# Down sums of three token blocks of a fused layer with the weights stationary and 512 tokens moving, their result transposed by DMA

## The chip, the cores and the metric

The kernel runs on one core of one Trainium2 chip. The metric is the device time of one execution in microseconds; lower is better. A profile also gives the *span*, from the first to the last recorded instruction of the core. The time is a little longer than the span, and that difference, which I call the *time outside the span*, becomes important below.

The engines are called PE (the matrix engine; "PEld" is its weight load), DVE (vector), ACT (activation), POOL and SP (which here mostly issues DMAs); SPq, ACTq and POOLq stand for these engines issuing DMAs. The trace also shows the clock that PE was granted, as a fraction of full speed.

Single executions of one kernel scatter by some tenths of a microsecond. A run is called slow when its granted clock is low; only fast runs, at granted clock 1.0 (two at 0.999), are compared in time here.

## The reference

For 2048 tokens of 640 channels, a layer norm feeds two branches, whose sum is added to the input:

```python
xn = _layernorm(x, axis=-1)
return x + _A_ref(xn, A_wqkv, A_wo) + _B_ref(xn, B_w_gate, B_w_up, B_w_down)

# _A_ref: 32 heads of 20 channels, each token attends to 8 tokens at distances 0, 2, ... 14; then @ wo
# _B_ref:
g = jnp.einsum("bsd,df->bsf", x, w_gate)      # 640 -> 1536
u = jnp.einsum("bsd,df->bsf", x, w_up)
return jnp.einsum("bsf,fd->bsd", g * u, w_down)   # 1536 -> 640
```

The last matrix products of both branches, `@ wo` (contraction 640, five pieces of 128) and `w_down` (contraction 1536, twelve pieces of 128), are summed in one accumulation of 17 matmuls. These are the *down sums*.

## The kernel before

All large products run on PE in bf16. Activations lie transposed in SBUF (channels on partitions, tokens along the free dimension). The down sums want their result with tokens on partitions, as the output in memory has it, so the kernel keeps a piece of 128 tokens of the activations stationary and moves 320 columns of the weights:

```python
# constants: TS = 128 (token tile), JB = 512 (token block), NF = 12, NCH = 5, DHALF = 320, TLAST = 12
def tail(t, nb):                      # tile t of 16, half nb of the 640 output channels
    j, rows = t // 4, slice((t % 4) * TS, (t % 4 + 1) * TS)
    flush_h(0)
    n = NF + NCH
    # ... (the very last half is cut into 192 + 128 columns)
        for i in range(n):
            if i < NF:
                l, x = ht(j, i)[:, rows], WD[:, i, cols]
            else:
                l, x = VO[:, i - NF, t * TS:(t + 1) * TS], WO[:, i - NF, cols]
            op("pe", ... e.matmul(PS[:, b, 0:wid], l, x, start=(i == 0), stop=(i == n - 1)) ...)
        if t < TLAST:
            if nb == 0:
                fin_bank[0] = b
                continue
            # both halves evicted together by ACT, fp16
            op("act", ... e.activation(o, i, ACT.Copy) ...)        # FACC <- PS, 128x640
            continue
        # tiles 12 to 15: DVE adds the input x and stores
    if nb == 1 and t < TLAST:
        if t % 2 == 0:
            return
        # two tiles together are added to the output in memory, which already holds a copy of x
        stores.append(op("pool", lambda e: e.dma_start(d, f, accum_op=ALU.add), ...))
```

A small layer in the kernel records every operation with what it reads and writes and derives all waits from that. Each DMA gets a semaphore of its own. The order of PE's work is a fixed list; a down sum of tile `t` is put behind the value block (the weighted sum of the attention, 256 tokens each, on DVE) that it reads:

```python
def add_dn(j):
    for t in range(4 * j, 4 * j + 4):
        for nb in range(2):
            fill.append(("dn", t // 2, 2.31, lambda t=t, nb=nb: tail(t, nb)))

add_gu(0); add_gu(1); add_gu(2)      # gate and up sums of a block of 512 tokens
add_dn(0); add_gu(3); add_dn(1); add_dn(2); add_dn(3)
```

Of the kernel before, what the change touches and what calls it, by code (L numbers as in the profile page):

```python
# [5 lines left out]
FP16 = mybir.dt.float16  # L6
ACT = mybir.ActivationFunctionType
ALU = mybir.AluOpType

S = 2048  # L10
D = 640
NCH = 5
# [3 lines left out]
NF = 12  # L16
W = 8
# [3 lines left out]
NJ = 4  # L21
TS = 128
JB = 512
# [6 lines left out]
SB = 256  # L30
NSB = HS // SB
# [10 lines left out]
class Sched:  # L42
# [50 lines left out]
    def op(self, eng, fn, r=(), w=(), dma=False, name="", group=None):  # L93
        X = _Op()
        X.eng, X.fn, X.name, X.dma = eng, fn, name, dma
        X.needs_tick, X.event, X.pre_know, X.idx = False, None, None, len(self.ops)
        rk = [k for a in r for k in self.keys(a)]
        wk = [k for a in w for k in self.keys(a)]
        deps = {}
        inorder = eng in ("pe", "act", "dve")  # L100
        for k in rk:
            st = self.state.get(k)
            if st is not None:
                for o in st[0]:
                    deps[o.idx] = o
        for k in wk:
            st = self.state.get(k)
            if st is None:
                continue
            if group is not None and st[2] == group and not st[1]:  # L110
                for o in st[3]:
                    deps[o.idx] = o
                continue
            for o in st[0]:
                if not (eng == "pe" and o.eng == "pe"):
                    deps[o.idx] = o
            for q in st[1]:
                if eng in ("pe", "act") and q.eng == eng and not q.dma:
                    continue
                deps[q.idx] = q  # L120
        last = {}
        keep = []
        for d in deps.values():
            if d.dma or d.eng == "pool":
                keep.append(d)
            else:
                b = last.get(d.eng)
                if b is None or b.idx < d.idx:
                    last[d.eng] = d
        X.deps = keep + list(last.values())  # L130
        for d in X.deps:
            if not d.dma:
                d.needs_tick = True
        for k in rk:
            st = self.state.get(k)
            if st is None:
                self.state[k] = [[], [X], None, []]
            elif inorder and st[1] and st[1][-1].eng == eng and not st[1][-1].dma:
                st[1][-1] = X
            else:  # L140
                st[1].append(X)
        for k in wk:
            st = self.state.get(k)
            if group is not None and st is not None and st[2] == group and not st[1]:
                st[0].append(X)
            else:
                before = [] if st is None else st[0] + st[1]
                self.state[k] = [[X], [], group, before]
        if dma:
            X.event = (self.nc.alloc_semaphore(f"dma{self.n_dma}"), 16)  # L150
            self.n_dma += 1
        self.ops.append(X)
        return X
# [59 lines left out]
def build_kernel(nc, A_x, A_wqkv, A_wo, B_x, B_w_gate, B_w_up, B_w_down, out):  # L213
    K = Sched(nc)
    op = K.op

    place = [16512]

    def sb(name, shape, dtype=BF16, at=None):
        n = mybir.dt.size(dtype)  # L220
        for s in shape[1:]:
            n *= s
        n = (n + 63) // 64 * 64
        if at is None:
            at = place[0]
            place[0] += n
        assert at + n <= 229344, (name, at + n)
        return K.sbuf(name, shape, dtype, at)
# [4 lines left out]
    WD = sb("WD", [128, NF, D])  # L233
    WO = sb("WO", [128, NCH, D])
# [9 lines left out]
    VO = sb("VO", [128, NCH, VP + S])  # L244
    QH, KH, ATB = [], [], []
# [25 lines left out]
    TLAST = 12  # L271
    XR = sb("XR", [128, NXR, D])
    NFO = 4
    FOUT = sb("FOUT", [128, NFO, D])
    FACC = sb("FACC", [128, NFO, D], FP16, at=place[0] - NFO * D * 2)
    NUS = 7
    a_us = place[0]
    USX = sb("USX", [128, NUS, JB])
# [9 lines left out]
    PS = nc.alloc_psum_tensor("PS", [128, 8, 512], FP32)  # L288
    xhbm = A_x[0]
    ohbm = out[0]  # L290

    def dma(o, i, r=(), w=(), name="", eng="sp", group=None):
        return op(eng, lambda e: e.dma_start(o, i), r=r, w=w, dma=True, name=name, group=group)
# [6 lines left out]
                                         fill=1.0, base=0, channel_multiplier=1),  # L300
       r=[IDENT[:]], w=[IDENT[:]], name="ident")
# [156 lines left out]
    def bank():  # L458
        b = bank_ring.pop(0)
        bank_ring.append(b)  # L460
        return b
# [164 lines left out]
    def flush_h(keep):  # L626
        n = 0
        while len(h_pending) > keep:
            h_pending.pop(0)()
            n += 1  # L630
        return n

    def ht(j, m):
        if j != 2:
            return HT[:, j % 3 % 2, m, :]
        if m < 2 * NCH:
            return XNT[:, m % NCH, m // NCH * JB:(m // NCH + 1) * JB]
        return HX[:, m - 2 * NCH, :]
# [19 lines left out]
    def xr_load(t):  # L658
        dma(XR[:, t % NXR, :], xhbm[t * TS:(t + 1) * TS, :], w=[XR[:, t % NXR, :]], name=f"xr{t}")

    stores = []
    fin_bank = [0]

    def tail(t, nb):
        j, rows = t // 4, slice((t % 4) * TS, (t % 4 + 1) * TS)
        flush_h(0)
        n = NF + NCH
        last = t == NT - 1
        parts = ((0, DHALF - 128), (DHALF - 128, 128)) if last and nb == 1 else ((0, DHALF),)
        for h, wid in parts:  # L670
            b = bank()
            c0 = nb * DHALF + h
            cols = slice(c0, c0 + wid)
# [4 lines that stand above are left out]
                    l, x = VO[:, i - NF, t * TS:(t + 1) * TS], WO[:, i - NF, cols]  # L678
                op("pe", (lambda l, x, i, b, wid: lambda e: e.matmul(PS[:, b, 0:wid], l, x, start=(i == 0), stop=(i == n - 1)))(l, x, i, b, wid),  # L679
                   r=[l, x], w=[PS[:, b, :]], name=f"dn{t}_{nb}_{i}")  # L680
            if t < TLAST:
                if nb == 0:
                    fin_bank[0] = b
                    continue
                assert b == fin_bank[0] + 1
                o = FACC[:, t % NFO, :].rearrange("p (n d) -> p n d", n=2)
                i = PS[:, b - 1:b + 1, 0:wid]
                op("act", (lambda o, i: lambda e: e.activation(o, i, ACT.Copy))(o, i),  # L688
                   r=[PS[:, b - 1, :], PS[:, b, :]], w=[o], name=f"fin{t}")
                continue  # L690
            o = FOUT[:, t % NFO, cols]
            xr = XR[:, t % NXR, cols]
            op("dve", (lambda o, xr, b, wid: lambda e: e.tensor_tensor(o, PS[:, b, 0:wid], xr, ALU.add))(o, xr, b, wid),  # L693
               r=[PS[:, b, :], xr], w=[o], name=f"fin{t}_{nb}")
            if last:
                eng = "act" if c0 == DHALF else "sp"
                stores.append(dma(ohbm[t * TS:(t + 1) * TS, cols], o, r=[o], name=f"odma{t}_{c0}", eng=eng))
        if nb == 1 and t < TLAST:
            if t % 2 == 0:
                return  # L700
            f = FACC[:, (t - 1) % NFO:(t - 1) % NFO + 2, :]
            d = ohbm[(t - 1) * TS:(t + 1) * TS, :].rearrange("(u p) n -> p u n", p=TS)
            stores.append(op("pool", lambda e: e.dma_start(d, f, accum_op=ALU.add), r=[f, ("out",)], w=[("out", t)],  # L703
                             dma=True, name=f"oacc{t}"))
        elif nb == 1 and not last:
            f = FOUT[:, t % NFO, :]
            stores.append(dma(ohbm[t * TS:(t + 1) * TS, :], f, r=[f], name=f"odma{t}"))
            if t + NXR < NT:
                xr_load(t + NXR)
# [84 lines left out]
    for which, t in ((0, 4), (1, 4), (0, 5), (1, 5)):  # L794
        b = bank()
# [19 lines left out]
    fill, pos = [], [0]  # L815
# [16 lines left out]
            fill.append((1.08, lambda m=m: glu(1, m, j)))  # L832

    def add_dn(j):
        for t in range(4 * j, 4 * j + 4):
            for nb in range(2):
                fill.append(("dn", t // 2, 2.31, lambda t=t, nb=nb: tail(t, nb)))

    add_gu(0)
    add_gu(1)  # L840
    add_gu(2)
    add_dn(0)
    add_gu(3)
    add_dn(1)
    add_dn(2)
    add_dn(3)

# [102 lines left out]
def bass_parallel_sum__sliding_local_dilated__glu_gated_bilinear__prompt_kernel(  # L950
    nc, A_x, A_wqkv, A_wo, B_x, B_w_gate, B_w_up, B_w_down, out
):
    build_kernel(nc, A_x, A_wqkv, A_wo, B_x, B_w_gate, B_w_up, B_w_down, out)
# [28 lines left out]
```

## Time and profile before

| | kernel before |
|---|---|
| time, fast runs at the start | 254.13 us median (253.92 to 254.18, 3 runs) |
| span of the profiled run, granted clock | 375.0 us, 0.658 (a slow run) |
| PE, DVE, ACT busy in it | 371.7, 219.0, 114.5 us |

The profile is of an execution in which PE was granted about 0.65 of its clock for almost the whole span. It shows the order of things and the durations of the other engines (ACT's 128x512 evictions took 597 ns in it; DVE was busy 219.0 us in it), but PE's times have to be rescaled.

These are lines from the page of the kernel before: busy time and share of the span for each engine with the number of instructions, the granted clock in tenths over 40 slices, and the chain of work that ended last, by engine.

```profile
span 375.0 us, 3825 instructions
## 1 busy us (share of the span) xinstructions
PE 371.7 (99%) x1572; PEld 184.2 (49%) x1572; DVE 219.0 (58%) x255; ACT 114.5 (31%) x202; POOL 35.8 (10%) x44
...
PEclk8666666666666666666666666666666666666666
...
## 4 chain that ended last, share of the span: by engine, by line
PE 99%; DVE 0%; issue 0%
```

PE is the chain: 99% of the span is PE work that follows directly on PE work. Whatever is to shorten the kernel has to shorten that stream.

The same chain in order of time (start in us, length in us, what, number of matmuls). L489 are 128-column matmuls, L648 the gate and up sums with 512 columns, L679 the down sums with mostly 320.

```profile
23.43 8.12 PE PS L489 x100
...
105.00 117.50 PE PS L648 x360
222.50 27.81 PE PS L679 x136
250.31 39.17 PE PS L648 x120
289.48 83.23 PE PS L679 x425
```

The 360 matmuls of 512 took 326.4 ns each, the first 136 of 320 took 204.5 ns each: nearly the same time per column.

Two groups of the kernel before, by form (line, engine, operation, tiles, shapes, count | busy us, mean ns | idle time before, and what ended it): a weight load of the down sums and their eviction.

```profile
L679 PEld LDWEIGHTS PS<-WD,HT 128*128 128x128 bf16 x300 | 35.5, 120 | 24.1 <-issue 0.9
...
L688 ACT ACTIVATE FACC<-PS 128x640 f16<-128x640 f32 x12 | 8.4, 703 | 73.3 <-PE PS L679 73.3
```

### The profile page before, as it was taken

To read this page: it belongs to the slowest core of one execution; us is meant where nothing else is said; L and a number is where in the kernel's file an instruction comes from. 1 tells how busy PE (TensorE), PEld (TensorE's weight loads), DVE (VectorE), ACT (ScalarE), POOL (GpSimd) and SP (SyncE) were. 2 spreads that over 40 slices of the span, in tenths; PEclk is the share of its full clock that TensorE was granted. 3 is DMA by queue.
4 is the path that set the end of the run, shared out by engine and by line. 5 is a ranking of instruction groups with operands and counts; after the bars stand their busy time and mean duration, and the time that the engine had idled before them with its cause. 6 is when DMAs were issued, how large, how long until landed. Compare 5 with 4: busy or idle time off the path is not lost.

```text
span 375.0 us, 3825 instructions
## 1 busy us (share of the span) xinstructions
PE 371.7 (99%) x1572; PEld 184.2 (49%) x1572; DVE 219.0 (58%) x255; ACT 114.5 (31%) x202; POOL 35.8 (10%) x44
## 2 busy tenths in 40 slices
PE   8999999999999999999999999999999999999997
PEld 5998544444433333333333346553334556556555
DVE  5766899992017238967666432997846998000111
ACT  4544443333333344333333332113333001001000
POOL 0000012344000300111100000110000010010000
PEclk8666666666666666666666666666666666666666
DMA  7754696766100412453991000612000020220411
GB/s 218 217 115 84 181 361 148 129 120 120 20 0 2 92 20 82 149 107 71 251 344 18 0 1 0 180 80 35 2 0 0 0 37 0 35 37 0 72 35 35
DMA packets 25664, 31.83 MB, mean 85 GB/s; under 512 B 9872, under 2 KB 22160, under 8 KB 25616
## 3 DMA queue, kind: packets, MB, share of 16 engines
q1 hardware_dynamic: 19120, 22.16, 18.3%
q0 software_dynamic: 6240, 9.31, 15.7%
q8 instruction: 12, 0.20, 0.2%
q10 hardware_dynamic: 288, 0.13, 0.1%
q14 instruction: 4, 0.03, 0.0%
HBM read 14.42 MB, written 4.59 MB: 51 GB/s over the span
## 4 chain that ended last, share of the span: by engine, by line
PE 99%; DVE 0%; issue 0%
PE PS L648 42%; PE PS L679 30%; PE PS L474 17%; PE PS L509 4%; PE PS L502 2%; PE PS L489 2%; PE PS L452 1%; PE PS L433 0%; DVE FOUT L693 0%; DVE ZERO L296 0%; DVE EPSC L297 0%
## 5 line engine op out<-in xcount | busy, mean ns | idle before, releaser
L648 PE MATMUL PS<-XNT,WU 128*128 128x512 bf16 x240 | 87.3, 513 | 0.0
L648 PE MATMUL PS<-XNT,WG 128*128 128x512 bf16 x240 | 87.3, 513 | 0.0
L474 PE MATMUL PS<-XNT,WQKV 128*128 128x512 bf16 x200 | 65.4, 513 | 0.0
L679 PE MATMUL PS<-WD,HT 128*128 128x320 bf16 (+2 forms) x300 | 63.4, 382 | 0.0
L648 PEld LDWEIGHTS PS<-XNT,WG 128*128 128x128 bf16 x240 | 29.3, 122 | 48.8 <-issue 48.7
L648 PEld LDWEIGHTS PS<-XNT,WU 128*128 128x128 bf16 x240 | 29.0, 121 | 49.3 <-issue 49.3
L679 PEld LDWEIGHTS PS<-WD,HT 128*128 128x128 bf16 x300 | 35.5, 120 | 24.1 <-issue 0.9
L653 DVE TENSOR_TENSOR HT<-HT,USX 128x512 bf16<-128x512 bf16 x36 | 15.2, 422 | 54.8 <-ACT USX L650 54.8
L474 PEld LDWEIGHTS PS<-XNT,WQKV 128*128 128x128 bf16 x200 | 26.9, 135 | 38.0 <-issue 37.7
L615 DVE TENSOR_TENSOR PVB<-VO,ATB 128x10240 f16<-128x10240 bf16 x8 | 43.9, 5488 | 0.2
L650 ACT ACTIVATE USX<-PS 128x512 bf16<-128x512 f32 x48 | 28.6, 597 | 48.7 <-PE PS L648 47.7
L679 PE MATMUL PS<-WO,VO 128*128 128x320 bf16 (+2 forms) x165 | 38.8, 384 | 0.0
L610 DVE TENSOR_TENSOR PVB<-PVB 128x5120 f16<-128x5120 f16 (+1 forms) x16 | 34.5, 2155 | 0.3
L693 DVE TENSOR_TENSOR FOUT<-PS,XR 128x320 bf16<-128x320 f32 (+2 forms) x9 | 4.1, 454 | 51.7 <-PE PS L679 51.7
L650 ACT ACTIVATE HT<-PS 128x512 bf16<-128x512 f32 x36 | 21.5, 597 | 36.4 <-PE PS L648 36.4
L688 ACT ACTIVATE FACC<-PS 128x640 f16<-128x640 f32 x12 | 8.4, 703 | 73.3 <-PE PS L679 73.3
L543 POOL DMA_DIRECT2D LOG<-PE x24 | 21.9, 925 | 58.0 <-DMA LOG<-PE 58.0
L679 PEld LDWEIGHTS PS<-WO,VO 128*128 128x128 bf16 x165 | 19.7, 121 | 13.0
L703 POOL DMA_DIRECT2D out_dram<-FACC x6 | 7.1, 1186 | 141.9 <-ACT FACC L688 141.9
L532 DVE TENSOR_TENSOR PP<-QH,KH 128x2048 f16<-128x2048 bf16 x16 | 19.1, 1218 | 0.0
L532 DVE TENSOR_TENSOR TMP<-QH,KH 128x2048 f16<-128x2048 bf16 x16 | 19.0, 1218 | 0.0
L537 DVE TENSOR_TENSOR PP<-PP,TMP 128x4096 f16<-128x4096 f16 x8 | 18.3, 2289 | 0.2
(67 smaller groups left out, 250.6 us busy)
## 6 DMA issues: line engine op xcount, KB each, us to landing
PE<-PP POOLq DMA_DIRECT2D x8, 512.0 KB, 4.8
ATB<-LOG SPq DMA_DIRECT2D x8, 512.0 KB, 4.8
LOG<-PE POOLq DMA_DIRECT2D x24, 128.0 KB, 2.7
WG<-in_B_w_gate_dram SPq DMA_DIRECT2D x1, 1920.0 KB, 9.1
WU<-in_B_w_up_dram SPq DMA_DIRECT2D x1, 1920.0 KB, 15.8
WD<-in_B_w_down_dram SPq DMA_DIRECT2D x1, 1920.0 KB, 10.0
out_dram<-in_A_x_dram SPq DMA_DIRECT2D x1, 1920.0 KB, 9.1
out_dram<-FACC POOLq DMA_DIRECT2D x6, 320.0 KB, 4.8
```

What stands on the lines that cost most here:

```text
L474: op("pe", (lambda l, x, c: lambda e: e.matmul(PS[:, b, :], l, x, start=(c == 0), stop=(c == NCH - 1)))(l, x, c), r=[l, x], w=[PS[:, b, :] ...
L509: op("pe", (lambda l, x, c: lambda e: e.matmul(o, l, x, start=(c == 0), stop=(c == NCH - 1)))(l, x, c), r=[l, x], w=[o], name=f"pw{which}_ ...
L532: return (1.22, lambda: op("dve", lambda e: e.tensor_tensor(o, qw, kw, ALU.mult), r=[q, k], w=[o], name=f"prod{h}_{p}_{c}"))
L537: (2.3, lambda: op("dve", lambda e: e.tensor_tensor(a, a, b, ALU.add), r=[a, b], w=[a], name=f"psum{h}_{p}")),
L543: op("pool", lambda e: e.dma_start(o, i, accum_op=ALU.add), r=[o, i], w=[o], dma=True, name=name)
L610: return lambda: op("dve", lambda e: e.tensor_tensor(o, x, y, ALU.add), r=[x, y], w=[o], name=f"{name}_{b}")
L615: lambda: op("dve", lambda e: e.tensor_tensor(PVB[:], vw, aw, ALU.mult), r=[v, a], w=[PVB[:]], name=f"pv_{b}")),
L648: op("pe", (lambda l, x, c: lambda e: e.matmul(PS[:, b, :], l, x, start=(c == 0), stop=(c == NCH - 1)))(l, x, c), r=[l, x], w=[PS[:, b, :] ...
L650: op("act", lambda e: e.activation(o, PS[:, b, :], ACT.Copy), r=[PS[:, b, :]], w=[o], name=f"guev{which}_{m}_{j}")
L653: h_pending.append(lambda: op("dve", lambda e: e.tensor_tensor(h, h, o, ALU.mult), r=[h, o], w=[h], name=f"h{m}_{j}"))
L679: op("pe", (lambda l, x, i, b, wid: lambda e: e.matmul(PS[:, b, 0:wid], l, x, start=(i == 0), stop=(i == n - 1)))(l, x, i, b, wid), r=[l, ...
L688: op("act", (lambda o, i: lambda e: e.activation(o, i, ACT.Copy))(o, i), r=[PS[:, b - 1, :], PS[:, b, :]], w=[o], name=f"fin{t}")
```

## The change

The intent is fewer, wider matmuls. For the first three blocks of 512 tokens the operands swap roles: a 128x128 piece of the weights is stationary and 512 tokens move. A block then needs 5 x 17 = 85 matmuls of 512 columns instead of 8 x 17 = 136 of 320, so 153 matmuls and weight loads fewer over three blocks. The result comes out with channels on partitions, so each 128x512 piece is evicted as fp16 and transposed by a DMA issued from SP; the same accumulating stores then add it to the output. The fourth block stays as it was. The cut diff:

```diff
+    def down_t(j, d):
+        flush_h(0)
+        b = bank()
+        n = NF + NCH
+        cols, toks = slice(d * TS, (d + 1) * TS), slice(j * JB, (j + 1) * JB)
+        for i in range(n):
+            if i < NF:
+                l, x = WD[:, i, cols], ht(j, i)
+            else:
+                l, x = WO[:, i - NF, cols], VO[:, i - NF, toks]
+            op("pe", ... e.matmul(PS[:, b, :], l, x, start=(i == 0), stop=(i == n - 1)) ...)
+        o = DT[:, (NCH * j + d) % 4]
+        op("act", lambda e: e.activation(o, PS[:, b, :], ACT.Copy), r=[PS[:, b, :]], w=[o], name=f"fin{j}_{d}")
+        f = FACC[j][:, :, cols]
+        op("sp", lambda e: e.dma_start_transpose(f, o), r=[o], w=[f], dma=True, name=f"oT{j}_{d}")
+        if d < NCH - 1:
+            return
+        for u in range(0, NJ, 2):
+            # two accumulating stores from POOL for the block, as before
     def add_dn(j):
+        if j < NJ - 1:
+            for d in range(NCH):
+                fill.append(("dn", 2 * j + 1, 3.67, lambda d=d: down_t(j, d)))
+            return
         for t in range(4 * j, 4 * j + 4):
```

(Cut: the buffers DT and FACC, which lie in space that is free by then, and the removed lines of `tail` for tiles under 12.)

More of the change, by code (lines that the diff above doesn't have):

```diff
@@ L274, in build_kernel @@
     FOUT = sb("FOUT", [128, NFO, D])
-    FACC = sb("FACC", [128, NFO, D], FP16, at=place[0] - NFO * D * 2)
+    DT = sb("DT", [128, 4, JB], FP16, at=K.base[ATB[1].name] + NSB * W * SB * 2)
+    FACC = [sb(f"FACC{k}", [128, NJ, D], FP16, at=a) for k, a in
+            enumerate((place[0] - NFO * D * 2, K.base[ATB[0].name], K.base[ATB[0].name] + NJ * D * 2))]
     NUS = 7
@@ L661, in build_kernel @@
     stores = []
-    fin_bank = [0]
+    def down_t(j, d):
[8 more added lines that the diff above has]
+                l, x = WO[:, i - NF, cols], VO[:, i - NF, toks]
+            op("pe", (lambda l, x, i: lambda e: e.matmul(PS[:, b, :], l, x, start=(i == 0), stop=(i == n - 1)))(l, x, i),
+               r=[l, x], w=[PS[:, b, :]], name=f"dt{j}_{d}_{i}")
+        o = DT[:, (NCH * j + d) % 4]
[5 more added lines that the diff above has]
+        for u in range(0, NJ, 2):
+            f2 = FACC[j][:, u:u + 2]
+            t = NJ * j + u
+            h = ohbm[t * TS:(t + 2) * TS, :].rearrange("(u p) n -> p u n", p=TS)
+            stores.append(op("pool", (lambda h, f2: lambda e: e.dma_start(h, f2, accum_op=ALU.add))(h, f2), r=[f2, ("out",)],
+                             w=[("out", t)], dma=True, name=f"oacc{t}"))
     def tail(t, nb):
@@ L680, in tail @@
                    r=[l, x], w=[PS[:, b, :]], name=f"dn{t}_{nb}_{i}")
-            if t < TLAST:
-                if nb == 0:
-                    fin_bank[0] = b
-                    continue
-                assert b == fin_bank[0] + 1
-                o = FACC[:, t % NFO, :].rearrange("p (n d) -> p n d", n=2)
-                i = PS[:, b - 1:b + 1, 0:wid]
-                op("act", (lambda o, i: lambda e: e.activation(o, i, ACT.Copy))(o, i),
-                   r=[PS[:, b - 1, :], PS[:, b, :]], w=[o], name=f"fin{t}")
-                continue
             o = FOUT[:, t % NFO, cols]
@@ L697, in tail @@
                 stores.append(dma(ohbm[t * TS:(t + 1) * TS, cols], o, r=[o], name=f"odma{t}_{c0}", eng=eng))
-        if nb == 1 and t < TLAST:
-            if t % 2 == 0:
-                return
-            f = FACC[:, (t - 1) % NFO:(t - 1) % NFO + 2, :]
-            d = ohbm[(t - 1) * TS:(t + 1) * TS, :].rearrange("(u p) n -> p u n", p=TS)
-            stores.append(op("pool", lambda e: e.dma_start(d, f, accum_op=ALU.add), r=[f, ("out",)], w=[("out", t)],
-                             dma=True, name=f"oacc{t}"))
-        elif nb == 1 and not last:
+        if nb == 1 and not last:
             f = FOUT[:, t % NFO, :]
```

## The prediction

> **What bounds the kernel now.** TensorE. The chain of waits gives PE 99% of the span in one unbroken stream; the list of waits has no PE wait over 1.0 us. The profile ran at a lowered clock (mean granted 0.658, span 375.0 us); the timed runs took 254.13 us. [...] They are PE-bound too, but there the DVE (219 us busy) has much less slack than the profile shows.
>
> **What the change removes and adds.** Down sums of 12 token tiles: 408 matmuls of 320 columns become 255 of 512, 130,560 columns before and after. PE gains only what a matmul costs beyond its columns, 153 times.
> - In the chain, 136 matmuls of 320 took 27.81 us (204.5 ns each), 360 of 512 took 117.5 us (326.4 ns). A line through both gives about 1.3 ns per matmul plus 0.635 ns per column (estimate). [...]
> - Weight loads were hidden already. They show 120 ns each, but 128-column matmuls ran every 81 ns (100 in 8.12 us), so a load every 81 ns is possible[...]. Halving their density should gain nothing.
> - ACT: 12 evictions of 703 ns become 15 of about 597 ns; off the path.
> - 15 DMA transposes (the twelve in the kernel landed in 2.6 us each) go on the SP queue; the accumulating stores stay 6, 4.8 us each. The third block's land some 10 us after its last matmul; nearly 18 us of matmuls of the fourth block follow, so the kernel still ends with the last tile's add and store.
>
> **New waits.** Each 512-token sum needs both value blocks of its tokens at once: the first needs the second value block about 9 us of full-clock PE time earlier than before. In the throttled profile that block was ready at 211 us and the down sums began at 222.5. At full clock I added the trace's DVE durations in queue order, with matmuls rescaled: 3 us of slack are left at the first down block (11 before), 7 us or more at the others. The order of everything else on DVE and PE is unchanged. Three transposes stand ahead of the second half's attention moves on SP; two value blocks (21 us of DVE) lie between, so that should not show.
>
> **Prediction.** 254.13 - 0.4 = 253.8 us: range 253.0 to 255.0 (8 in 10), allowing a small wait. Faster by over 2%: 1%; within 2%: 96%; slower by over 2%: 3%.
>
> **What would show it.** Down sums with unchanged PE time per column (a profile at clock 0.65 should span about 374.8 us); weight-load busy time down by about 18 us (153 x 120 ns) with nothing gained; no PE wait on the value blocks; transposes landing in about 2.6 us; the last accumulating store landed well before the end.
>
> **What would make it wrong.** If 320-column matmuls at full clock are held by their weight loads, the gain is some us. If the second value block is late at full clock, PE waits 1 to 3 us and the change loses. If transposes are slow or block the SP queue, the accumulating stores slip, but they have some 8 us.

The gain was summed as 153 matmuls times the fixed cost of one, and came to 0.2 to 0.4 us: the lower end is 153 times the 1.3 ns fitted above. 0.4 us was at the time not shown by a trace; the fixed cost was measured later, as 2.5 ns (before_spare15 and the changed kernel, and n160).

The argument on weight loads compares a load every 81 ns with a matmul every 204.5 ns, both at the clock of the profile. From the trace alone, 0.635 ns per column at a mean granted clock of 0.658 would be 0.418 ns at full clock, and 581,000 columns 243 us of the 254.13 (my estimate, which takes the time to go inversely with the granted clock; 512 columns took 326.4 ns in this profile and 215.8 ns at clock 1.0). The other times at full clock in the prediction are estimates by rescaling as well: for the nearly 18 us of the fourth block 18.53 us were measured later (changed kernel), and the 9 us of PE time are close to half a block, 68 matmuls of 135.8 ns or 9.2 us (before_spare15).

## The result, and the profile after

| | before | after |
|---|---|---|
| time, median of 6 runs each | 254.16 us (253.89 to 254.24) | 254.19 us (253.91 to 254.63) |
| ratio of the fast runs, 95% interval | | 1.0005 (0.9992 to 1.0018) |
| span of the profiled run, granted clock | 375.0 us, 0.658 | 252.5 us, 1.0 |

A ratio is the mean time of one kernel's fast runs over that of the other's of the same rounds, so it is not quite the ratio of the medians. The result is correct and the time is the same. A gain of 0.4 us would be a ratio of 0.9984, which lies outside the interval.

The page of the changed kernel, the same lines:

```profile
span 252.5 us, 3530 instructions
## 1 busy us (share of the span) xinstructions
PE 247.8 (98%) x1400; PEld 134.8 (53%) x1419; DVE 215.2 (85%) x255; ACT 114.6 (45%) x205; POOL 35.9 (14%) x44
...
PEclk9999999999999999999999999999999999999999
...
## 4 chain that ended last, share of the span: by engine, by line
PE 96%; DMA 2%; SPq 1%; issue 1%; DVE 0%
```

This profile ran at full clock (mean granted 1.0; a 9 in the row PEclk is 90% or more), so PE's times can be read as they stand, but they can't be set against the slow profile of before. The chain in order of time:

```profile
12.29 1.12 PE PS L504 x20
...
18.86 5.58 PE PS L491 x100
...
150.77 8.63 PE PS L675 x40
159.40 0.05 issue
159.46 9.66 PE PS L675 x44
...
195.02 7.55 PE PS L675 x35
...
224.21 7.50 PE PS L675 x34
231.71 18.53 PE PS L705 x153
250.24 0.02 issue
250.26 0.29 DVE FOUT L709
```

A block of 85 matmuls begins at 150.77 and ends at 169.12, which is 215.9 ns each; the two others go from 195.02 to 231.71, 215.8 ns each. (In the long streams of 512-column matmuls of this trace one in 50 has no record, and PE has 1400 records in all against 1419 weight loads; the pieces of 0.05 us called issue stand where one is missing, so the start and end of a stretch, not the sum of its pieces, are the measure.) There is no wait between the sums. The 153 matmuls of the fourth block follow, and the kernel ends with the last tile's addition as before.

The groups that answer to those of before, and two lines of the list of DMAs (transfer, queue, kind, count, size, median us from issue to landing):

```profile
L678 ACT ACTIVATE DT<-PS 128x512 f16<-128x512 f32 x15 | 9.0, 597 | 43.6 <-PE PS L675 40.5 <-remote 3.1
...
L675 PEld LDWEIGHTS PS<-HT,WD 128*128 128x128 bf16 x120 | 11.7, 98 | 14.2
```

```profile
out_dram<-FACC POOLq DMA_DIRECT2D x6, 320.0 KB, 5.5
...
FACC<-DT SPq DMA_TRANSPOSE x15, 2.3
```

The new evictions and transposes are cheap: 597 ns each on ACT, and 2.3 us to landing. In the timeline of the changed kernel, POOL's issues of the accumulating stores (start, length, what, and the idle time before, which a transpose ended):

```profile
173.98 2.42 POOL L687 DMA_DIRECT2D out_dram<-FACC  x2 [23.12 <-DMA FACC<-DT]
216.61 2.39 POOL L687 DMA_DIRECT2D out_dram<-FACC  x2 [40.20 <-DMA FACC<-DT]
234.96 2.39 POOL L687 DMA_DIRECT2D out_dram<-FACC  x2 [15.96 <-DMA FACC<-DT]
```

The last pair is issued by 237.4 us. An accumulating store took 5.5 us to land in the median and 8.4 us at most, so they are done at least 6.7 us before the span ends at 252.5 (252.5 - 237.4 - 8.4).

The wait that I feared most was for the second value block. These lines are from two timelines of the changed kernel, DVE's and PE's: DVE finishes writing that block at 148.36 + 0.81 = 149.17 us, and the first matmuls that read values start at 153.20.

```profile
148.36 0.81 DVE L612 TENSOR_TENSOR VO<-PVB 128x1280 bf16<-128x1280 f16 x1
```

```profile
153.20 1.24 PE L675 MATMUL PS<-VO,WO 128*128 128x512 bf16 x5
```

4.0 us of slack were left, where 3 were estimated.

So nothing in the span of the changed kernel looks worse than predicted, and still the time did not fall. The question for the experiments was where 0.4 us went.

### The profile page after: what moved, and what is told of

The parts are those of the page before. It is cut to its first block, busy times and chain, and to the rows that moved or that the text cites. A ratio compares the mean times of both kernels' runs of the same rounds, so it can differ in the third digit from the quotient of the medians.

```text
span 252.5 us, 3530 instructions
## 1 busy us (share of the span) xinstructions
PE 247.8 (98%) x1400; PEld 134.8 (53%) x1419; DVE 215.2 (85%) x255; ACT 114.6 (45%) x205; POOL 35.9 (14%) x44
## 2 busy tenths in 40 slices
DMA packets 33824, 33.79 MB, mean 134 GB/s; under 512 B 18032, under 2 KB 30320, under 8 KB 33776
## 4 chain that ended last, share of the span: by engine, by line
PE 96%; DMA 2%; SPq 1%; issue 1%; DVE 0%
PE PS L650 41%; PE PS L675 22%; PE PS L476 17%; PE PS L705 7%; PE PS L511 4%; PE PS L491 2%; PE PS L504 2%; DMA WQKV<-in_A_wqkv_dram 2%; SPq L295 1%; PE PS L435 0%; DVE FOUT L709 0%
## 5 line engine op out<-in xcount | busy, mean ns | idle before, releaser
L650 PE MATMUL PS<-XNT,WU 128*128 128x512 bf16 x237 | 59.0, 379 | 0.2
L650 PE MATMUL PS<-XNT,WG 128*128 128x512 bf16 x232 | 57.9, 379 | 0.4
L476 PE MATMUL PS<-XNT,WQKV 128*128 128x512 bf16 x196 | 43.0, 379 | 0.2
L650 PEld LDWEIGHTS PS<-XNT,WU 128*128 128x128 bf16 x240 | 23.5, 98 | 28.3
L650 PEld LDWEIGHTS PS<-XNT,WG 128*128 128x128 bf16 x240 | 23.5, 98 | 28.3
L678 ACT ACTIVATE DT<-PS 128x512 f16<-128x512 f32 x15 | 9.0, 597 | 43.6 <-PE PS L675 40.5
L675 PE MATMUL PS<-HT,WD 128*128 128x512 bf16 x118 | 27.4, 379 | 0.1
L675 PEld LDWEIGHTS PS<-HT,WD 128*128 128x128 bf16 x120 | 11.7, 98 | 14.2
L675 PE MATMUL PS<-VO,WO 128*128 128x512 bf16 x74 | 18.4, 379 | 0.0
L545 POOL DMA_DIRECT2D PE<-PP x8 | 8.7, 1088 | 60.9 <-DVE PP L540 60.9
```

The costliest lines, as they stand in the source:

```text
L476: op("pe", (lambda l, x, c: lambda e: e.matmul(PS[:, b, :], l, x, start=(c == 0), stop=(c == NCH - 1)))(l, x, c), r=[l, x], w=[PS[:, b, :] ...
L545: op("pool", lambda e: e.dma_start(o, i, accum_op=ALU.add), r=[o, i], w=[o], dma=True, name=name)
L650: op("pe", (lambda l, x, c: lambda e: e.matmul(PS[:, b, :], l, x, start=(c == 0), stop=(c == NCH - 1)))(l, x, c), r=[l, x], w=[PS[:, b, :] ...
L675: op("pe", (lambda l, x, i: lambda e: e.matmul(PS[:, b, :], l, x, start=(i == 0), stop=(i == n - 1)))(l, x, i), r=[l, x], w=[PS[:, b, :]], ...
```

## The experiments

The kernel before ran again in the same rounds. The last two columns of the table are means over the fast runs; the time outside the span is the time minus the span.

| run | time, mean | ratio, 95% interval | span | outside |
|---|---|---|---|---|
| before, all 38 timed beside the experiments | 254.22 | | 252.43 | 1.79 |
| the changed kernel, first result (6) | 254.22 | 1.0005 (0.9992 to 1.0018) | 252.12 | 2.10 |
| before_again (4) | 254.10 | 0.9992 (0.9979 to 1.0006) | 252.32 | 1.78 |
| after_again (5) | 254.14 | 0.9994 (0.9981 to 1.0006) | 252.04 | 2.10 |
| n160 (5) | 255.17 | 1.0035 (1.0021 to 1.0049) | 253.38 | 1.79 |
| plain_copy (5) | 254.06 | 0.9991 (0.9978 to 1.0003) | 251.96 | 2.10 |
| before_spare15 (5) | 254.22 | 1.0002 (0.9990 to 1.0014) | 252.44 | 1.78 |
| after_recycle_oT (6) | 254.14 | 0.9999 (0.9987 to 1.0010) | 252.07 | 2.07 |
| before_recycle (5) | 254.20 | 1.0001 (0.9989 to 1.0013) | 252.42 | 1.78 |
| after_recycle (5) | 254.14 | 1.0000 (0.9987 to 1.0013) | 252.04 | 2.10 |
| before_sp_nops (5) | 254.43 | 1.0007 (0.9994 to 1.0019) | 252.62 | 1.81 |
| before_act_nops (5) | 254.24 | 0.9999 (0.9987 to 1.0012) | 252.46 | 1.78 |
| after_oT_act (5) | 254.12 | 0.9996 (0.9983 to 1.0010) | 252.04 | 2.08 |
| no_transposes (5) | 253.79 | 0.9987 (0.9974 to 1.0001) | 251.98 | 1.81 |

Times of single executions scatter with a standard deviation of about 0.2 us, so a difference of a few tenths is at the edge of what a ratio can show. Several of these ratios can't tell 0.9985, which a theory forecast, from 1: the intervals of after_again, plain_copy and after_oT_act hold both. The time outside the span is far steadier: each value lies between 1.73 and 1.86 us, or between 2.04 and 2.15 us, and nothing lies between, although the record gives spans only to 0.1 us. So the theories are judged by it.

### The two kernels once more

before_again and after_again are the two kernels unchanged.

> The kernel before, unchanged, once more, to get its profile at full clock and to see how far two equal kernels differ. Theory A (the matmul saving is real, 153 x 2.6 ns = 0.4 us, and something else of the same size takes it back): the down sums of the first twelve tiles run at 136 ns per 320-column matmul, and this trace shows less time than the changed kernel somewhere else. Theory B (there is no saving at full clock): 320-column matmuls run at 133 to 134 ns, so the twelve tiles take about 54.5 us instead of the 55.0 us of the 512-column form. Theory C (the saving is there, and hidden by the scatter of the first 7.5 us, which wait for loads): 136 ns, all else equal, and the start differs from run to run by some tenths of a us. Ratio to before: 1.000, within 0.0015.

> The changed kernel, unchanged, five more rounds on one chip beside the others. Theory A and B: ratio 1.000 within 0.001. Theory C: 0.9985 once the scatter is averaged out (0.4 us faster).

The figures of the theories can be worked out from the trace of the changed kernel. Its 128-column matmuls took 55.8 ns each (100 in 5.58 us) and those of 512 columns 215.8 ns, which is 0.4167 ns per column and 2.5 ns per matmul. So 320 columns would take 133.3 ns without the fixed cost and 135.8 ns with it (estimates).

The profiled run of before_again was slow again (granted clock 0.561, span 440.2 us), so it gave no profile at full clock (what lowers the clock in such runs is not shown here); before_spare15 below, in which every instruction is that of before, stands in for it. The timed runs gave the clue instead. In the same rounds the changed kernel's span was 252.04 us against 252.50 us for the kernel before, but its time outside the span was 2.10 us against 1.80. Theory B was left to the next run, and C was half right: the start does scatter. Theory A turned out right in a form I had not thought of: the loss is not in the span at all.

The chain of before_spare15 in order of time, for comparison with that of the changed kernel:

```profile
12.14 1.12 PE PS L503 x20
...
18.72 5.58 PE PS L490 x100
...
150.63 18.47 PE PS L680 x136
...
195.00 55.48 PE PS L680 x425
...
250.50 0.29 DVE FOUT L694
```

The 136 matmuls of the first block took 18.47 us, 135.8 ns each. All down sums took 18.47 + 55.48 = 73.95 us; in the changed kernel they took 18.35 + 36.69 + 18.53 = 73.57 us. The 0.38 us between them are the 153 matmuls, 2.5 ns each. Before the down sums the streams are alike: 128-column matmuls take 5.58 us per 100 in both. The scatter lies ahead of them: the first line of each fence, the last of the short matmuls that wait for loads, ends at 13.26 us here and at 13.41 us in the changed kernel (and at 12.80 us in the next fence), and from there on the streams run without a wait.

### Narrower matmuls

```diff
-            for i in range(n):
+            for k0, kw in (((0, 160), (160, 160)) if t < TLAST else ((0, wid),)):
+                for i in range(n):        # matmul into PS[:, b, k0:k0 + kw]
```

> The kernel before with every 320-column matmul of the first twelve tiles cut into two of 160: 408 matmuls more, the same columns. If a matmul costs 2.6 ns beyond its columns (theories A and C), 408 x 2.6 = 1.06 us slower, ratio 1.0042. If the fixed cost does not exist in the down sums (theory B), under 0.3 us slower. If weight loads hold short matmuls, several us slower.

The two halves are accumulated one after the other. The run was 0.88 us slower in span than the kernel before in the same rounds (253.38 against 252.50 over five and nine runs). Its chain in order of time:

```profile
11.68 1.12 PE PS L502 x20
...
150.19 18.81 PE PS L681 x272
...
194.91 56.16 PE PS L681 x697
...
251.09 0.29 DVE FOUT L695
```

The first block took 18.81 us against 18.47, and the rest 56.16 against 55.48: together 1.02 us for 408 matmuls, 2.5 ns each (the 0.88 us of the mean spans differ from it by less than the start scatters). This rules theory B out: the fixed cost exists in the down sums, with 160 as with 320 columns. The weight loads were doubled too and cost no more than these 2.5 ns, so weight loads do not hold 320-column matmuls. Every matmul of these kernels has a load of its own, so no run here can say whether the 2.5 ns belong to the matmul or to its load.

### The transposes replaced by plain copies

```diff
-        op("sp", lambda e: e.dma_start_transpose(f, o), ...)
+        op("sp", lambda e: e.dma_start(f, o.rearrange("p (u c) -> p u c", u=NJ)), ...)
```

> The changed kernel with each DMA transpose replaced by a plain copy of the same bytes to the same place (wrong result on purpose): the matmul part of the change without the transposes. Theory A with the transposes as what takes the saving back: 0.4 us faster than before, ratio 0.9985. Otherwise the same as the changed kernel within 0.1%.

The result is wrong, as said. The span was 251.96 us and the time outside 2.10 us, as in the changed kernel. So it is not the transposing that costs time outside the span.

### Semaphores

The changed kernel has 15 DMAs more, and so 15 semaphores more (122 for DMAs instead of 107). If the semaphores were the cause, 0.3 us for 15 would promise about a microsecond for a kernel that makes do with 60 (estimate). One kernel allocates 15 more and does not use them; three kernels recycle them, after_recycle_oT for the 15 transposes alone, before_recycle and after_recycle throughout:

```diff
 # before_spare15
+        self.spare = [nc.alloc_semaphore(f"spare{i}") for i in range(15)]
 # after_recycle_oT, before_recycle, after_recycle: at the point where waits are worked out
+            if X.dma:
+                free = [q for q in pool if kn.get(q, 0) >= pool[q]] if ... else []
+                sem = free[0] if free else nc.alloc_semaphore(...)
+                # the event counts on from what the semaphore already holds
```

The condition `...` is "a transpose of a down sum" for after_recycle_oT and "not issued from POOL" for the other two; the DMAs of POOL keep a semaphore each. A semaphore is taken again only by an engine that knows that its earlier DMAs have landed.

> The kernel before with 15 more semaphores allocated and never used; every instruction as before. So far the time outside the span (time minus span) is 1.75 to 1.8 us for the kernel before and for its form with 160 columns, and 2.06 to 2.13 us for the changed kernel and its form with plain copies. Theory S (the time outside the span grows with the number of the highest semaphore): 2.1 us here, and 0.35 us slower than before. Theory U (it grows with the semaphores that are used) and theory D (it grows with the DMAs or descriptors of the SP queue): 1.78 us, no slower.

> The changed kernel with the 15 transposes counted on semaphores of loads that landed long ago, so as many semaphores as before; the DMAs as in the changed kernel. Theories S and U: time outside the span 1.78 us, so 0.35 us faster than the changed kernel and 0.38 us faster than before (253.8 us, ratio 0.9985). Theory D: 2.1 us outside the span, time as the changed kernel.

> The kernel before with 60 DMA semaphores instead of 107: every DMA of SP and ACT counts on a semaphore whose earlier DMAs its engine knows to have landed. Theories S and U, at 0.35 us for 15: 47 fewer are worth 1.1 us, time outside the span about 0.7 us, ratio 0.9957. Theory D: nothing.

> The changed kernel with 60 DMA semaphores instead of 122. Theories S and U: time outside the span as in the kernel before with 60 (about 0.7 us), and 0.38 us faster than that one by the matmuls: ratio 0.994 to before. Theory D: as the changed kernel, 2.1 us outside the span.

Every form of before kept 1.78 us outside the span, with 107 semaphores, with 15 more, or with 60. Every form of the changed kernel kept 2.07 to 2.10, with 107 or with 60. Theories S and U both fall; theory D (the DMAs) stayed.

### The length of the instruction programs

In the DMA records of the traces, an instruction fetch of 8 KB begins 1.1 us after the last instruction of before_spare15 and of the other forms of before, but 12 us before the last instruction of after_again (12.7 us in the first profile of the changed kernel). That made me guess that the length of the programs might matter. Two kernels were to lengthen the programs of SP and ACT with empty instructions, and one moves the transposes from SP to ACT:

```diff
 # before_sp_nops (30 on "sp"), before_act_nops (13 on "act")
+    for k in range(30):
+        op("sp", lambda e: e.nop(), name=f"nop{k}")
 # after_oT_act
-        op("sp", lambda e: e.dma_start_transpose(f, o), ...)
+        op("act", lambda e: e.dma_start_transpose(f, o), ...)
```

In after_oT_act two engines issue transposes. The twelve from SP are issued from 14.2 to 32.5 us and landed in 4.3 us at most, more than 100 us before the first from ACT at 154.5 us, and the result was correct; no run here had transposes from both in flight together.

> The kernel before with 30 empty instructions on SP in the middle of the kernel, so that the SP program has 150 instructions as in the changed kernel (120 before: 15 transposes and 15 waits less). So far the time outside the span is 1.78 us in every form of the kernel before and 2.07 to 2.10 us in every form of the changed kernel, whatever the semaphores. In the traces the 8 KB instruction fetch that comes about 1.2 us after the last instruction of the kernel before comes some 10 us before the end in the changed kernel. Theory P-SP (the time outside the span is set by the length of the SP program): 2.1 us outside, 0.3 us slower than before, ratio 1.0013. Theory P-ACT, or that the DMAs themselves cost it: 1.78 us and no slower.

> The kernel before with 13 empty instructions on ACT, so that the ACT program has 459 instructions as in the changed kernel (446 before). Theory P-ACT: 2.1 us outside the span, 0.3 us slower. Theory P-SP or the DMAs themselves: 1.78 us.

> The changed kernel with its 15 transposes issued from ACT instead of SP: SP has 120 instructions as before, ACT 489. All transposes of the layer norm, issued from SP, have landed long before the first of these. Theory P-SP: 1.78 us outside the span with the span of the changed kernel (252.05 us), so 253.8 us, ratio 0.9985: faster than both. Theory P-ACT or the DMAs themselves: 2.1 us outside, as the changed kernel.

The first two tell nothing. Their traces hold as many records of SP (78) and of ACT (246) as before, and the late fetch stands where it stood. When the two kernels are built again their programs have as many instructions as before (79 for SP, 246 for ACT); so the empty instructions never reached the program. Their 1.81 and 1.78 us outside the span are only two more repetitions of the kernel before. The third does tell: SP again had 78 records and the fetch again came 1.1 us after the last instruction, yet 2.08 us stayed outside the span. So neither the length of SP's program nor the place of that fetch is the cause.

### No transposes at all

```diff
-        op("act", ... e.activation(DT piece, PS[:, b, :], ACT.Copy) ...)
-        op("sp", lambda e: e.dma_start_transpose(f, o), ...)
+        i = PS[:, b, :].rearrange("p (u c) -> p u c", u=NJ)
+        op("act", lambda e: e.activation(f, i, ACT.Copy), ...)     # straight into FACC, wrong layout
```

> The changed kernel without its 15 transposes: ACT writes the down sums straight to where the transposed ones belong (wrong result on purpose, same stores). The empty instructions of the last runs left no trace of themselves in the records, and moving the transposes to ACT left 2.08 us outside the span, so the length of the SP program is not it, and semaphores are not. Theory T (the 15 DMAs or the waits they bring on ACT and POOL cost the 0.3 us outside the span): 1.78 us outside, span 252.05 us, time 253.8 us, ratio 0.9985. Theory P-PE (the shorter PE program does it): 2.1 us outside, 254.15 us, ratio 0.9997. The span should be that of the changed kernel in both.

The span was 251.98 us, as in the changed kernel, and the time outside it was 1.81 us, as in the kernel before. The time was 253.79 us against 254.17 in the same rounds: 0.38 us less, ratio 0.9987, with an interval that just reaches 1. The program of PE is the shorter one here, so PE's program length is not the cause. What costs 0.3 us outside the span are the 15 DMAs, transposing or plain, from SP or from ACT, or what they bring on ACT and POOL: waits, and with them longer programs. The changed kernel has 256 records of ACT and 61 of POOL, no_transposes 245 and 56, the kernel before 246 and 56. As the empty instructions of before_act_nops did not reach the program, no run separates these lengths from the DMAs.

This is a diagnostic, not a better kernel, since its result is wrong. No correct kernel that I tried was faster than the one before by more than the noise.

## Why the prediction was right

The measured 254.19 us lie within 253.0 to 255.0 and "within 2%" is right, but the forecast 0.4 us did not appear in the time. Range and verdict would have held without any gain, so they say little about the 0.4 us; what speaks for the argument is that its parts can be found in the traces. Point by point:

- **PE bounds the kernel, in the timed runs too.** Right. At full clock the chain of before_spare15 is one PE stream from 7.55 to 250.48 us, but for 0.04 us.
- **Columns cost the same, and 153 matmuls fewer gain 0.4 us.** Right, in the span: 0.38 us by the chains of before_spare15 and of the changed kernel. Over all fast runs the span fell from 252.43 (38 runs) to 252.08 us (11 runs), 0.35 us. At full clock 55.8 ns for 128 columns, 135.8 for 320 and 215.8 for 512 lie on a line of 0.4167 ns per column and 2.5 ns per matmul; n160 gives 2.5 ns too. The 1.3 ns fitted to the slow profile did not carry over.
- **Weight loads were hidden.** Right. n160 doubled them for twelve tiles and paid only the 2.5 ns per matmul with its load. Their busy time fell from 149.1 us (before_spare15) to 134.8, by 14.3 us instead of 18, mainly because a load of the down sums takes 98 ns at full clock and not the 120 of the slow profile. Nothing was gained by it.
- **Evictions, transposes and stores off the path.** Right. Evictions took 597 ns; transposes landed in 2.3 us in the median and 5.6 us at most, where 2.6 were expected; stores in 5.5 us in the median instead of 4.8, with at least 6.7 us to spare.
- **No PE wait on the value blocks, 3 us of slack.** Right: 4.0 us at the first block. (The forecast span of 374.8 us at a clock of 0.65 was not tested, as the profile ran at full clock.)
- **"254.13 - 0.4 = 253.8 us".** This step was wrong by its missing term. It took the time to fall with the span. The 15 added DMAs cost 0.31 us outside the span (2.10 against 1.79), and 0.35 of span less 0.31 leaves 0.04 us, which is the difference of the mean times (254.22 to 254.18), far within their scatter. That they, or what they bring on ACT and POOL, cost it is shown by no_transposes.

What stays open: whether it is the DMAs themselves, the packets they add (33,824 packets in the changed kernel against 25,664, 33,584 with plain copies), their waits on ACT and POOL, or the longer programs of these two; and whether the 0.31 us lie ahead of the first recorded instruction or behind the last. In the traces of the kernel before and of the changed kernel, only fetches of instructions begin outside the span, the first 10.7 us ahead of it and the last 1.1 us behind it, and these do not show it.

## What to carry to other kernels

At full clock, fewer and wider matmuls with the same columns gained 2.5 ns here for each matmul saved and no more, with the weight loads hidden; count that first, since 153 of them are 0.4 us of 254. When a predicted gain of tenths of a microsecond shows in the span and not in the time, subtract the one from the other for every run: what lies outside the span was steadier here (within 0.13 us for either kind of kernel, where single times scatter with a standard deviation of 0.2 us), and fifteen added DMAs, with their waits, took back 0.31 us there, nearly the 0.35 us that the matmuls had given. The profile at a granted clock of 0.658 was good for order and for slack on other engines (3 us estimated from it, 4.0 us measured), but the fixed cost fitted to it, 1.3 ns, did not hold at full clock, where it was 2.5 ns.
